# Linear attention into a spectral mixer: the last mode sum and its copies in halves, an eleventh unit for GpSimd, and another order of the last outputs

## The chip, the cores and the metric

One core of a Trainium2 chip. The metric is the device time of one execution in microseconds (us), the median of several runs. The engines are TensorE (PE; PEld is its weight load), VectorE (DVE), ScalarE (ACT), GpSimd (POOL) and SyncE (SP, which only issues DMAs here). Sixteen DMA engines move data between the chip's memory and the SBUF; matmul results arrive in PSUM, which holds eight banks of 2 KB per partition.

## The reference

```python
def _attn_ref(q, k, v, w_phi):            # q, k, v: (8, 8, 576, 64), w_phi: (64, 128)
    def phi(x):
        proj = np.einsum('bhsd,df->bhsf', x, w_phi)
        proj = proj - np.max(np.abs(proj), axis=-1, keepdims=True)
        return np.concatenate([np.exp(proj), np.exp(-proj)], axis=-1)
    q_p, k_p = phi(q), phi(k)
    kv = np.einsum('bhsf,bhsd->bhfd', k_p, v)
    z = np.sum(k_p, axis=2)
    num = np.einsum('bhsf,bhfd->bhsd', q_p, kv)
    den = np.einsum('bhsf,bhf->bhs', q_p, z)[..., None] + 1e-06
    return num / den

def _moe_ref(x, w_r, w_i, w_ch):          # x: (8, 576, 512), w_r, w_i: (64, 512, 512)
    X = np.fft.rfft(x, axis=1)
    Y = np.zeros_like(X)
    Xr, Xi = np.real(X[:, :64]), np.imag(X[:, :64])
    Yr = np.einsum('bmd,mde->bme', Xr, w_r) - np.einsum('bmd,mde->bme', Xi, w_i)
    Yi = np.einsum('bmd,mde->bme', Xr, w_i) + np.einsum('bmd,mde->bme', Xi, w_r)
    Y[:, :64] = Yr + 1j * Yi
    y = np.fft.irfft(Y, n=576, axis=1)
    u = x + y
    return u + np.maximum(u @ w_ch, 0.0)
```

The attention's output, with its heads side by side, is the x of the second function. The weights `w_r` and `w_i` are 134 MB in float32; they are read once.

## The kernel before, in words

The kernel has one program for all engines with an order written out by hand.

**Attention.** 32 steps go over pairs of batches or heads. Each step makes the features of q and k, the sums over k, the quotient, and its part of the forward Fourier transform (`x_mm`). The result x stays in the SBUF as `xs_all`, 40 chunks of 128 rows: chunk `b * 5 + c` is rows of batch b, and the fifth chunk of a batch has only 64 rows.

**Mode sums.** 32 of them (k = 0 to 31): `weights(k)` loads a `wr` and a `wi` tile on the GpSimd queue, three sums ahead; `mode_mm` multiplies them with the transformed x into psY; `mode_sum` adds psY to `Yacc`. The sums 24 to 31 are the last ones of their eight groups of modes; there `mode_sum` writes the total as `yst` (bf16), TensorE transposes it into ptY, and VectorE copies ptY into `sY`. The first 22 sums run inside the attention, the others in a loop of their own behind it.

**By batch.** `by_batch(sY, P)` runs after k = 25, 27, 29 and 31 (P = 0 to 3). For its 16 modes it makes two things for each batch: Z, the spectrum times `w_ch` (`mm_z` into psZ), and Y, the spectrum itself (`mm_r` into psR). PSUM holds the batches j = 0 to 3 (and j + 4 in the second half, h = 1) in four groups of 32 partitions. ScalarE copies Z into `zall` and VectorE copies Y into `yall`, where each batch has its own columns and each P its own 32 rows. For P = 3 the copies of batches 0 and 4 go straight there; the others go through the staging tiles `stz` and `sty` and six DMAs of 64 KB, on SP for j = 1 and on GpSimd's queue for j = 2 and 3.

**Work in between.** In the same loop `pieces` transposes two chunks of x (`flip_x`, T3), multiplies them with `w_ch` (`times_w`, psW in T2) and lets ScalarE put the product into `xw`. `reordered` permutes the rows of a pair of chunks of `xs_all` in place: two matmuls into psX (T0 or T1) and one ScalarE copy (L686, L688). It is called up to twice after k <= 24 and after even k, and stops when the pair has not been through `flip_x` yet.

**Output units.** 20 units, four pairs of chunks and one half unit (the 64-row chunks of two batches) for each of b = 0 to 3, that is for batches b and b + 4. A unit adds the inverse transform of Z to `xw` in psB (`add_xw`, `add_z`), ScalarE takes its ReLU; it adds the inverse transform of Y to x in psA (`add_x`, `spec`), and VectorE adds psA to the ReLU. In a "late" unit, whose pair is listed in `late`, x does not go through TensorE: GpSimd adds the reordered x at the end (L778). psB and psA of even and odd units lie in T2, T3 and T0, T1. The outputs are issued on SP (L856); `lag` says how many units later the issue stands. The groups b = 1 and b = 2 write four chunks with one DMA, b = 0 and b = 3 two.

Four PSUM tags, T0 to T3, of two banks each, hold everything behind the attention. An access waits for the earlier accesses of the same tile that it depends on.

Of the kernel before, what the change touches and what calls it, by code (L numbers as in the profile page):

```python
# [10 lines left out]
F32 = mybir.dt.float32  # L11
F32R = mybir.dt.float32r
BF16 = mybir.dt.bfloat16
I32 = mybir.dt.int32
ACT = mybir.ActivationFunctionType
ALU = mybir.AluOpType
AX = mybir.AxisListType

B_, H_, S_, D_ = 8, 8, 576, 64
NMODES = 64  # L20
DMODEL = 512
# [5 lines left out]
def kernel(  # L27
# [11 lines left out]
    nc = tc.nc  # L39
# [4 lines left out]
    psum = psum_cm.__enter__()  # L44
    pw = ctx.enter_context(tc.tile_pool(name="pw", bufs=3))

    ident_b = const.tile([128, 128], BF16, name="ident_b")
# [8 lines left out]
    Yacc = pers.tile([128, 8, DMODEL], F32, name="Yacc")  # L56
# [333 lines left out]
    def mode_mm(k, tag="yr"):  # L390
        g, gi = groups[k]
        XT = XTs[1 - g if k < 8 else g % 2]
        wt = W.pop(k)
        if gi < 0:
            psY = psum.tile([128, 2, DMODEL], F32, name="psY2", tag="pC", bufs=1)
            for par in range(2):
                for ri in range(2):
                    for j in range(4):
                        for x in range(2):
                            r = slice(64 * x, 64 * x + 64)  # L400
                            m = 16 * (-1 - gi) + 8 * x + 2 * j + par
                            c0 = (16, 0, 48, 32)[2 * ri + par]
                            nc.tensor.matmul(
                                psY[32 * j:32 * j + 32, x, :],
                                lhsT=XT[r, c0:c0 + 32, m],
                                rhs=wt[ri][r, 2 * j + par, :],
                                start=(par == 0 and ri == 0), stop=(par == 1 and ri == 1),
                            )
            return psY
        psY = psum.tile([128, DMODEL], F32, name="psY", tag=tag, bufs=1)  # L410
        for par in range(2):
            for ri in range(2):
                for j in range(4):
                    m = 8 * gi + 2 * j + par
                    c0 = (16, 0, 48, 32)[2 * ri + par]
                    nc.tensor.matmul(  # L416
                        psY[32 * j:32 * j + 32, :],
                        lhsT=XT[:, c0:c0 + 32, m],
                        rhs=wt[ri][:, 2 * j + par, :],
                        start=(par == 0 and ri == 0), stop=(par == 1 and ri == 1),  # L420
                    )
        return psY

    def mode_sum(k, psY, pb=None):
        g, gi = groups[k]
        if gi < 0:
            G = -1 - gi
            if g == 0:
                nc.vector.tensor_copy(Yacc[:, 2 * G:2 * G + 2, :], psY)
            else:  # L430
                nc.vector.tensor_tensor(
                    out=Yacc[:, 2 * G:2 * G + 2, :], in0=psY, in1=Yacc[:, 2 * G:2 * G + 2, :],
                    op=ALU.add)
        elif g < 3:
            nc.vector.tensor_tensor(  # L435
                out=Yacc[:, gi, :], in0=psY, in1=Yacc[:, gi, :], op=ALU.add)
        else:
            yst = pb.tile([128, DMODEL], BF16, name="yst", tag="yst", bufs=2)
            nc.vector.tensor_tensor(out=yst, in0=psY, in1=Yacc[:, gi, :], op=ALU.add)
            return yst  # L440


# [76 lines left out]
    psY = None  # L519
# [3 lines left out]
    with tc.manual_schedule():  # L523
# [25 lines left out]
        for n in range(N + 2):  # L549
# [9 lines left out]
            if psY is not None:  # L559
                mode_sum(k_out, psY)  # L560
                psY = None
# [70 lines left out]

    yall = pb.tile([128, B_, DMODEL], BF16, name="yall", bufs=1)
    zall = pb.tile([128, B_, DMODEL], BF16, name="zall", bufs=1)
    xw = pb.tile([128, B_ * NCH - N_EARLY, DMODEL], BF16, name="xw", bufs=1)


# [2 lines left out]
    copies = []  # L642
# [20 lines left out]
    def pieces(n):  # L663
        for _ in range(n):
# [7 lines left out]
                copies.pop(0)()  # L672


    late = {0: ((1, 0), (1, 2)), 1: ((0, 0), (1, 0), (1, 2)), 2: ((0, 0), (1, 0), (1, 2)),
            3: ((0, 0), (0, 2))}
    reorder = sorted((b + 4 * x) * NCH + c for b in range(4) for x, c in late[b])

    def reordered(tag):
# [10 lines left out]

    def by_batch(sY, P):
        cols = [sY[:, dc].rearrange("p g c -> p (g c)") for dc in range(4)]
        psZ = psum.tile([128, 2, DMODEL], F32, name="psZ", tag="T0")
        psR = psum.tile([128, 2, DMODEL], F32, name="psR", tag="T1")

        def mm_z(h):
            for dc in range(4):
                for j in range(4):
                    nc.tensor.matmul(psZ[32 * j:32 * j + 32, h, :], lhsT=cols[dc][:, j + 4 * h::8],  # L699
                                     rhs=wchb[:, dc, :], start=(dc == 0), stop=(dc == 3))  # L700

        def mm_r(h):
            for dc in range(4):
                for j in range(4):
                    nc.tensor.matmul(
                        psR[32 * j:32 * j + 32, h, dc * 128:(dc + 1) * 128],
                        lhsT=cols[dc][:, j + 4 * h::8], rhs=ident_b, start=True, stop=True)

        rows = slice(32 * P, 32 * P + 32)

        def copy(j):
            r = slice(32 * j, 32 * j + 32)
            nc.scalar.copy(zall[rows, j::4, :], psZ[r])
            nc.vector.tensor_copy(yall[rows, j::4, :], psR[r])  # L714

        if P < 3:
            for f in (mm_z, mm_r):
                for h in range(2):
                    f(h)
            copies.extend([lambda j=j: copy(j) for j in range(4)])  # L720
            return

        stz, sty = [pb.tile([128, 2, DMODEL], BF16, name=nm, bufs=1) for nm in ("stz", "sty")]
        for h in range(2):
            mm_z(h)
            mm_r(h)
            nc.scalar.copy(zall[rows, 4 * h, :], psZ[0:32, h, :])
            nc.vector.tensor_copy(yall[rows, 4 * h, :], psR[0:32, h, :])  # L730
        nc.scalar.copy(stz, psZ)
        nc.vector.tensor_copy(sty, psR)
        for j in range(1, 4):
            for dst, src in ((zall, stz), (yall, sty)):
                (nc.sync if j == 1 else nc.gpsimd).dma_start(
                    dst[rows, j::4, :], src[32 * j:32 * j + 32])

# [43 lines left out]
    with tc.manual_schedule():  # L783
        plan = {22: 3, 23: 3, 24: 2, 25: 2, 26: 2, 27: 1, 28: 2, 29: 1, 30: 1, 31: 0}
        while k_out < 32:
            k = k_out
            gi = groups[k][1]
            while k_in < min(k_out + NW, 32):
                weights(k_in)
                k_in += 1  # L790
            if k == 31:
                add_xw(u0)
            yst = mode_sum(k, mode_mm(k, "T3"), pb)
            k_out += 1
            if yst is not None:
                if ahead:
                    times_w()
                pt = psum.tile([128, 4, 128], BF16, name="ptY", tag="T3" if k < 31 else "T1")
                for dc in range(4):
                    nc.tensor.transpose(pt[:, dc, :], yst[:, dc * 128:(dc + 1) * 128], ident_b)  # L800
                if k == 31:
                    add_x(u0)
                if gi % 2 == 0:
                    sY = pb.tile([128, 4, 2, 128], BF16, name="sY", tag="sY")
                nc.vector.tensor_copy(sY[:, :, gi % 2, :], pt)
                if gi % 2 == 1:
                    by_batch(sY, gi // 2)
            pieces(plan[k])
            if k <= 24 or k % 2 == 0:
                assert not copies  # L810
                for tag in ("T0", "T1"):
                    if reorder:
                        reordered(tag)
            if k == 30:
                times_w()
        assert not todo and not ahead and not reorder and not copies

    units = []
    for b in range(4):
# [4 lines left out]
        for x in range(2):  # L824
            out_v = out[b + 4 * x].rearrange("(p n) e -> p n e", n=9)
            for c in (0, 2):
# [8 lines left out]
        u4 = dict(bc=((b, 4), (b + 4, 4)), o=o4, late=False, half=True, lag=0,  # L835
                  dmas=[(out[b + 4 * x].rearrange("(p n) e -> p n e", n=9)[:, 4, :],
                         o4[64 * x:64 * x + 64]) for x in range(2)])
        units += [u4] + us if b == 3 else us + [u4]
    units[0].update(psA=u0["psA"], psB=u0["psB"])

    with tc.manual_schedule():
        for n, u in enumerate(units):
            u["tags"] = ("T2", "T3") if n % 2 == 0 else ("T0", "T1")
        for n in range(len(units) + 3):
            if n < len(units):
                u = units[n]
                if n:
                    add_xw(u)
                add_z(u)
                if n:  # L850
                    add_x(u)
                spec(u)
            for lag in (3, 1, 0):
                if 0 <= n - lag < len(units) and units[n - lag]["lag"] == lag:
                    for dst, src in units[n - lag]["dmas"]:
                        nc.sync.dma_start(dst, src)  # L856


# [28 lines left out]
```

## Time and profile before

| | |
|---|---|
| median of 3 runs | 457.19 us (456.78, 457.19, 460.01) |
| profiled execution | 456.96 us, its span 455.2 us |
| busy in the span | TensorE 305.3 us (67%), VectorE 295.8 (65%), ScalarE 261.2 (57%), GpSimd 196.9 (43%) |
| moved by DMA | 97.70 MB, mean 215 GB/s as written; memory reads 163.64 MB |
| GpSimd adds L778 | 10 of 2.13 us, 425.4 to 448.8 |
| final adds L774 | 16 of 1.22 us and 4 of 0.68 us, 421.15 to 448.9 |
| last output issue on SP | 451.59 us |

The span runs from the first to the last instruction of the profiled execution; 1.76 us lie around it. A row of a timeline has the start, the time from the first start to the last end, the engine, the line, the operation, the output and inputs, the shapes, the number of instructions, and in brackets the idle time before it with what ended it. A row of the chain has the start, its length and what it was. A row of the stretches has the window, its length, the busy time and number of instructions of each engine, the granted TensorE clock, the mean busy share of the DMA engines (it can read above 1) and the rate.

### The profile page before, as it was taken

What the parts mean: (1) busy time and instruction counts of PE and PEld (TensorE: products, weight loads), DVE (VectorE), ACT (ScalarE), POOL (GpSimd) and SP (SyncE); (2) the same over time, 40 slices, a digit from 0 to 9 for tenths busy, and PEclk for the clock granted to TensorE, in tenths of its full rate; (3) what the DMA queues carried; (4) which work ended last, traced back from release to release, by engine and by line L of the source; (5) the groups of instructions that cost most, each with busy time, mean ns of one, the idle gap of its engine ahead of it and who ended that gap; (6) DMA issues with size and microseconds to landing.
All of it is one profiled execution on the core that took longest, in us unless ns stands there. A gap on an engine that the chain in (4) does not pass through costs nothing.

```text
span 455.2 us, 11075 instructions
## 1 busy us (share of the span) xinstructions
PE 305.3 (67%) x4637; PEld 199.0 (44%) x4637; DVE 295.8 (65%) x417; ACT 261.2 (57%) x528; POOL 196.9 (43%) x250
## 2 busy tenths in 40 slices
PE   3476686745676676657564554776678878867993
PEld 2364565633554554534443332543344445444441
DVE  6588789847988788876657472776422362654873
ACT  4576877833676877865545452766224455554662
POOL 4956576445564356644344341444011311100793
PEclk9998889876779879996678685988899999999998
DMA  6999999999999999999999999999999999990787
GB/s 182 191 229 222 225 216 226 221 206 225 216 225 218 229 219 227 220 221 223 222 208 219 219 218 218 207 208 208 207 207 207 207 207 208 206 187 15 242 325 299
DMA packets 84034, 97.70 MB, mean 215 GB/s; under 512 B 3281, under 2 KB 77265, under 8 KB 83473
## 3 DMA queue, kind: packets, MB, share of 16 engines
q0 software_dynamic: 75728, 76.75, 101.4%
q1 hardware_dynamic: 8096, 20.19, 12.6%
q8 instruction: 36, 0.59, 0.5%
q14 instruction: 14, 0.11, 0.1%
q10 hardware_dynamic: 160, 0.07, 0.1%
HBM read 163.64 MB, written 9.44 MB: 380 GB/s over the span
## 4 chain that ended last, share of the span: by engine, by line
DMA 30%; PE 24%; DVE 24%; ACT 8%; issue 6%; POOL 5%; SPq 1%; DVEq 0%; ACTq 0%; POOLq 0%
DMA wi<-in_moe_w_i_dram 14%; DMA k<-in_k_dram 6%; DVE mkq L233 6%; PE psW L659 6%; DMA wr<-in_moe_w_r_dram 5%; DMA q<-in_q_dram 5%; DVE xs_all L336 3%; DVE nd L322 3%; DVE tB L315 3%; ACT AA L240 2%; PE psY L416 2%; POOL vaug L270 2%; PE psZ L699 2%; DVE yall L714 2%; ACT e L262 2%
## 5 line engine op out<-in xcount | busy, mean ns | idle before, releaser
L270 POOL TENSOR_TENSOR vaug<-vn,ee 128x576 bf16<-128x576 f32 x64 | 72.8, 1156 | 57.2 <-ACT ee L255 45.7
L240 ACT ACTIVATE AA<-psT 128x1024 bf16<-128x1024 f32 x64 | 62.0, 1021 | 42.8 <-PE psT L208 42.3
L162 POOL DMA_DIRECT2D wr<-in_moe_w_r_dram x24 | 21.9, 912 | 114.2 <-PE psY L416 107.9
L262 ACT ACTIVATE e<-mkq 64x4 f32<-64x4 f32 (+1 forms) x128 | 26.3, 206 | 63.1 <-DVE mkq L233 60.8
L244 ACT ACTIVATE AA<-psk 128x1024 bf16<-128x1024 f32 x64 | 61.4, 1009 | 0.0
L416 PE MATMUL psY<-wi,XT 128*32 128x512 bf16 x192 | 24.8, 464 | 25.0 <-DMA wi<-in_moe_w_i_dram 25.0
L416 PEld LDWEIGHTS <-XT 128*32 128x32 bf16 x384 | 17.7, 167 | 51.9 <-issue 43.4
L233 DVE TENSOR_REDUCE mkq<-psk 128x8 f32<-128x1024 f32 x32 | 38.8, 1213 | 1.0 <-PE psk L199 0.9
L233 DVE TENSOR_REDUCE mkq<-psq 128x8 f32<-128x1024 f32 x32 | 38.9, 1217 | 0.5 <-PE psq L199 0.4
L435 DVE TENSOR_TENSOR Yacc<-psY,Yacc 128x512 f32<-128x512 f32 x16 | 11.0, 689 | 42.2 <-PE psY L416 42.2
L661 ACT CAST xw<-psW 128x1024 bf16<-128x1024 f32 x17 | 17.2, 1012 | 36.4 <-PE psW L659 30.5
L286 PE MATMUL kvz<-vaug,AA 64*128 64x65 bf16 x1152 | 29.7, 212 | 11.4 <-POOL vaug L275 10.1
L190 DVE COPY kT<-ptr 128x640 bf16<-128x640 bf16 x32 | 15.7, 492 | 32.4 <-PE ptr L184 32.4
L416 PE MATMUL psY<-wr,XT 128*32 128x512 bf16 x192 | 24.5, 469 | 16.3 <-DMA wr<-in_moe_w_r_dram 7.5
L315 DVE TENSOR_TENSOR tB<-psNB,e 128x650 f32<-128x650 f32 x32 | 26.7, 833 | 11.6 <-PE psNB L305 11.0
L659 PE MATMUL psW<-wchb,sT 128*128 128x512 bf16 x136 | 32.2, 379 | 2.1 <-ACT xw L661 2.1
L286 PEld LDWEIGHTS <-AA 64*128 64x128 bf16 x1152 | 25.6, 108 | 16.2 <-issue 12.4
L305 PEld LDWEIGHTS <-AA 128*128 128x128 bf16 x640 | 28.7, 109 | 8.8 <-issue 8.5
L336 DVE TENSOR_TENSOR xs_all<-nd,rden 128x640 bf16<-128x640 f32 x32 | 29.5, 921 | 1.1
L208 PE MATMUL psT<-qT,w 64*128 64x512 bf16 x64 | 15.4, 471 | 21.0 <-DVE mkq L233 21.0
L322 DVE TENSOR_TENSOR nd<-psNA,tB 128x650 f32<-128x650 f32 x32 | 26.7, 835 | 4.1 <-DVE tB L315 0.5
L184 PE MATMUL ptr<-ident_b,k 128*128 128x128 bf16 x160 | 17.6, 254 | 14.8 <-DVE qT L190 13.0
(135 smaller groups left out, 712.2 us busy)
## 6 DMA issues: line engine op xcount, KB each, us to landing
wr<-in_moe_w_r_dram POOLq DMA_DIRECT2D x24, 1024.0 KB, 23.6
wi<-in_moe_w_i_dram POOLq DMA_DIRECT2D x24, 1024.0 KB, 27.8
wr<-in_moe_w_r_dram POOLq DMA_DIRECT2D x16, 512.0 KB, 16.1
wi<-in_moe_w_i_dram POOLq DMA_DIRECT2D x16, 512.0 KB, 19.4
vn<-in_v_dram SPq DMA_DIRECT2D x24, 288.0 KB, 5.6
out_dram<-of SPq DMA_DIRECT2D x16, 256.0 KB, 2.4
out_dram<-of SPq DMA_DIRECT2D x8, 512.0 KB, 3.7
q<-in_q_dram POOLq DMA_DIRECT2D x12, 288.0 KB, 20.0
```

Of the source, the lines that this page charges most:

```text
L233: nc.vector.tensor_reduce(out=o, in_=i, axis=AX.X, op=ALU.max, apply_absolute_value=True)
L240: nc.scalar.activation(AA[:, 0, ab, 0:1024].rearrange("f (x j p) -> f j x p", j=2, p=64), st["psT"].rearrange("f j (x p) -> f j x p", p=64 ...
L244: nc.scalar.activation(AA[:, 1, ab, 0:1024].rearrange("p (c j f) -> p j c f", c=4, j=2), st["psk"], ACT.Exp, scale=sc)
L262: nc.scalar.activation(e2[64 * jj:64 * jj + 64, hh, 0:NCH - jj], mkq[64 * hh:64 * hh + 64, 1, 5 * jj:5 + 4 * jj], ACT.Exp, scale=2.0)
L270: nc.gpsimd.tensor_tensor(out=vaug[:, ab, :, 0:64], in0=st["v"], in1=ee[:, ab, :].unsqueeze(2).to_broadcast([128, 9, D_]), op=ALU.mult,)
L286: nc.tensor.matmul(kvz[:, hh, ab * 65:(ab + 1) * 65], lhsT=AA[r, 1, ab, 128 * j:128 * j + 128], rhs=vaug[r, ab, j, :], start=(j == 0), sto ...
L305: nc.tensor.matmul(p[:, hh, 65 * c:65 * c + 65], lhsT=AA[:, 0, ab, x:x + 128], rhs=kvzF[:, hh, ab * 65:(ab + 1) * 65], start=True, stop=True,)
L315: nc.vector.tensor_tensor(out=tB, in0=st["psNB"], in1=e2.unsqueeze(3).to_broadcast([128, 2, NCH, 65]), op=ALU.mult,)
L322: nc.vector.tensor_tensor(out=nd, in0=st["psNA"], in1=st["tB"], op=ALU.add)
L336: nc.vector.tensor_tensor(out=xo, in0=nd[:, :, :, 0:64], in1=rden.to_broadcast([128, 2, NCH, 64]), op=ALU.mult,)
L416: nc.tensor.matmul(psY[32 * j:32 * j + 32, :], lhsT=XT[:, c0:c0 + 32, m], rhs=wt[ri][:, 2 * j + par, :], start=(par == 0 and ri == 0), sto ...
L659: nc.tensor.matmul(ps[:, x, :], lhsT=sT[:, x, dc, :], rhs=wchb[:, dc, :], start=(dc == 0), stop=(dc == 3))
```

## The change

- `mode_mm` runs over `ri` (wr or wi) in its outer loop and over the parity of the mode in its inner one.
- At k = 31 `mode_sum` adds in two halves of 256 columns into two tiles; the transposes go into two PSUM tiles (T0 and T1) and each is copied on its own.
- `yall` and `zall` become two halves of one tile `zy`. `by_batch` no longer has psZ and psR: there is one tile for each half h of the batches, with Z in its first bank and Y in its second. For P < 3 ScalarE copies Z and Y of the first half, VectorE those of the second. For P = 3 the order of the matmuls stays; the staging tile of the first half is copied by ScalarE as soon as that half is there, that of the second by VectorE, and each DMA moves Z and Y of one batch.
- `late[0]` gains (0, 2): an eleventh late unit, and an eleventh pair to reorder.
- The half unit of b = 3 is the last unit instead of the first of its group.
- From the last unit's step on, the second output of a unit is issued on ScalarE's queue.

```diff
-        for par in range(2):
-            for ri in range(2):
+        for ri in range(2):
+            for par in range(2):
                 for j in range(4):
...
-            yst = pb.tile([128, DMODEL], BF16, name="yst", tag="yst", bufs=2)
-            nc.vector.tensor_tensor(out=yst, in0=psY, in1=Yacc[:, gi, :], op=ALU.add)
+            cuts = [0, DMODEL] if k < 31 else [0, DMODEL // 2, DMODEL]
+            yst = []
+            for a, b in zip(cuts, cuts[1:]):
+                t = pb.tile([128, b - a], BF16, name="yst", tag="yst" if k < 31 else f"yst{a}",
+                            bufs=2 if k < 31 else 1)
+                nc.vector.tensor_tensor(out=t, in0=psY[:, a:b], in1=Yacc[:, gi, a:b], op=ALU.add)
+                yst += [t[:, x:x + 128] for x in range(0, b - a, 128)]
...
-    late = {0: ((1, 0), (1, 2)), 1: ((0, 0), (1, 0), (1, 2)), 2: ((0, 0), (1, 0), (1, 2)),
-            3: ((0, 0), (0, 2))}
+    late = {0: ((0, 2), (1, 0), (1, 2)), 1: ((0, 0), (1, 0), (1, 2)),
+            2: ((0, 0), (1, 0), (1, 2)), 3: ((0, 0), (0, 2))}
...
-        psZ = psum.tile([128, 2, DMODEL], F32, name="psZ", tag="T0")
-        psR = psum.tile([128, 2, DMODEL], F32, name="psR", tag="T1")
+        ps = [psum.tile([128, 2, DMODEL], F32, name="psZY", tag=f"T{h}") for h in range(2)]
...
-        def copy(j):
-            r = slice(32 * j, 32 * j + 32)
-            nc.scalar.copy(zall[rows, j::4, :], psZ[r])
-            nc.vector.tensor_copy(yall[rows, j::4, :], psR[r])
+        def copy(j, h, eng):
+            eng(zy[rows, :, j + 4 * h, :], ps[h][32 * j:32 * j + 32])
 
         if P < 3:
-            for f in (mm_z, mm_r):
-                for h in range(2):
-                    f(h)
-            copies.extend([lambda j=j: copy(j) for j in range(4)])
+            for h in range(2):
+                mm_z(h)
+                mm_r(h)
+            copies.extend([lambda j=j: (copy(j, 0, nc.scalar.copy),
+                                        copy(j, 1, nc.vector.tensor_copy)) for j in range(4)])
             return
-        stz, sty = [pb.tile([128, 2, DMODEL], BF16, name=nm, bufs=1) for nm in ("stz", "sty")]
         for h in range(2):
             mm_z(h)
             mm_r(h)
-            nc.scalar.copy(zall[rows, 4 * h, :], psZ[0:32, h, :])
-            nc.vector.tensor_copy(yall[rows, 4 * h, :], psR[0:32, h, :])
-        nc.scalar.copy(stz, psZ)
-        nc.vector.tensor_copy(sty, psR)
-        for j in range(1, 4):
-            for dst, src in ((zall, stz), (yall, sty)):
+            nc.scalar.copy(zall[rows, 4 * h, :], ps[h][0:32, 0, :])
+            nc.vector.tensor_copy(yall[rows, 4 * h, :], ps[h][0:32, 1, :])
+            st = pb.tile([128, 2, DMODEL], BF16, name=f"st{h}", bufs=1)
+            (nc.vector.tensor_copy if h else nc.scalar.copy)(st, ps[h])
+            for j in range(1, 4):
                 (nc.sync if j == 1 else nc.gpsimd).dma_start(
-                    dst[rows, j::4, :], src[32 * j:32 * j + 32])
+                    zy[rows, :, j + 4 * h, :], st[32 * j:32 * j + 32])
...
-                pt = psum.tile([128, 4, 128], BF16, name="ptY", tag="T3" if k < 31 else "T1")
-                for dc in range(4):
-                    nc.tensor.transpose(pt[:, dc, :], yst[:, dc * 128:(dc + 1) * 128], ident_b)
+                if gi % 2 == 0:
+                    sY = pb.tile([128, 4, 2, 128], BF16, name="sY", tag="sY")
+                for a, b, tag in ((0, 4, "T3"),) if k < 31 else ((0, 2, "T0"), (2, 4, "T1")):
+                    pt = psum.tile([128, b - a, 128], BF16, name="ptY", tag=tag)
+                    for dc in range(a, b):
+                        nc.tensor.transpose(pt[:, dc - a, :], yst[dc], ident_b)
+                    nc.vector.tensor_copy(sY[:, a:b, gi % 2, :], pt)
                 if k == 31:
                     add_x(u0)
...
-        units += [u4] + us if b == 3 else us + [u4]
+        units += us + [u4]
...
-                    for dst, src in units[n - lag]["dmas"]:
-                        nc.sync.dma_start(dst, src)
+                    for x, (dst, src) in enumerate(units[n - lag]["dmas"]):
+                        (nc.scalar if x and n >= len(units) - 1 else nc.sync).dma_start(dst, src)
```

More of the change, by code (lines that the diff above doesn't have):

```diff
@@ L630 @@
     psum = ctx.enter_context(tc.tile_pool(name="psumT", bufs=1, space=bass.MemoryType.PSUM))
-    yall = pb.tile([128, B_, DMODEL], BF16, name="yall", bufs=1)
-    zall = pb.tile([128, B_, DMODEL], BF16, name="zall", bufs=1)
+    zy = pb.tile([128, 2, B_, DMODEL], BF16, name="zy", bufs=1)
+    zall, yall = zy[:, 0], zy[:, 1]
     xw = pb.tile([128, B_ * NCH - N_EARLY, DMODEL], BF16, name="xw", bufs=1)
@@ L698, in mm_z @@
                 for j in range(4):
-                    nc.tensor.matmul(psZ[32 * j:32 * j + 32, h, :], lhsT=cols[dc][:, j + 4 * h::8],
+                    nc.tensor.matmul(ps[h][32 * j:32 * j + 32, 0, :], lhsT=cols[dc][:, j + 4 * h::8],
                                      rhs=wchb[:, dc, :], start=(dc == 0), stop=(dc == 3))
@@ L705, in mm_r @@
                     nc.tensor.matmul(
-                        psR[32 * j:32 * j + 32, h, dc * 128:(dc + 1) * 128],
+                        ps[h][32 * j:32 * j + 32, 1, dc * 128:(dc + 1) * 128],
                         lhsT=cols[dc][:, j + 4 * h::8], rhs=ident_b, start=True, stop=True)
         rows = slice(32 * P, 32 * P + 32)
-        def copy(j):
-            r = slice(32 * j, 32 * j + 32)
-            nc.scalar.copy(zall[rows, j::4, :], psZ[r])
-            nc.vector.tensor_copy(yall[rows, j::4, :], psR[r])
+        def copy(j, h, eng):
+            eng(zy[rows, :, j + 4 * h, :], ps[h][32 * j:32 * j + 32])
         if P < 3:
-            for f in (mm_z, mm_r):
-                for h in range(2):
-                    f(h)
-            copies.extend([lambda j=j: copy(j) for j in range(4)])
+            for h in range(2):
[3 more added lines that the diff above has]
+                                        copy(j, 1, nc.vector.tensor_copy)) for j in range(4)])
             return
-        stz, sty = [pb.tile([128, 2, DMODEL], BF16, name=nm, bufs=1) for nm in ("stz", "sty")]
         for h in range(2):
@@ L797 @@
                     times_w()
-                pt = psum.tile([128, 4, 128], BF16, name="ptY", tag="T3" if k < 31 else "T1")
-                for dc in range(4):
-                    nc.tensor.transpose(pt[:, dc, :], yst[:, dc * 128:(dc + 1) * 128], ident_b)
+                if gi % 2 == 0:
[5 more added lines that the diff above has]
+                    nc.vector.tensor_copy(sY[:, a:b, gi % 2, :], pt)
                 if k == 31:
                     add_x(u0)
-                if gi % 2 == 0:
-                    sY = pb.tile([128, 4, 2, 128], BF16, name="sY", tag="sY")
-                nc.vector.tensor_copy(sY[:, :, gi % 2, :], pt)
                 if gi % 2 == 1:
```

## The prediction

> Unit numbers below follow the last loop of the changed program: u0 to u4 for batches 0 and 4, u5 to u9, u10 to u14, u15 to u19; the fifth of each group is the 64-row unit, which the kernel before runs first in the last group.
>
> **What bounds the kernel now.** I read the stretches first, then the chain that ended last, then the timeline of each engine from 395 us on, then the output tiles.
>
> ```profile
> core 0: us, PE busy (x) PEld busy (x) DVE busy (x) ACT busy (x) POOL busy (x), PEclk, DMA share, GB/s
> 395.00:405.00 10.00, 8.68 (x124) 5.36 (x123) 4.28 (x6) 5.36 (x6) 0.00 (x0) 1.00 1.24 208
> ...
> 412.00:420.00 8.00, 6.11 (x92) 3.63 (x92) 2.95 (x5) 2.25 (x4) 0.00 (x0) 1.00 0.02 4
> ...
> 430.00:440.00 10.00, 9.82 (x53) 4.13 (x53) 7.94 (x8) 7.27 (x8) 8.67 (x5) 1.00 0.83 320
> ```
>
> Up to 405 the DMA engines are full (share 1.24) with weights. From 412 to 420 they are idle: nothing is loaded any more and nothing is ready to be written. From 420 the output units run and TensorE is busy 98%. Every edit that can matter lies behind 340 us.
>
> ```profile
> 349.50 1.89 PE psW L659 x8
> 351.39 0.43 PE psX L686 x2
> 351.82 1.05 PE psY L416 x15
> ...
> 411.27 1.02 ACT xw L661
> 412.30 0.04 issue
> 412.34 0.59 PE psB L751 x2
> 412.93 1.08 PE psY L416 x14
> 414.01 0.02 issue
> 414.03 0.70 DVE yst L439
> ```
>
> The chain shows that from 343 us to the last mode sum TensorE, VectorE and ScalarE hand work to each other and no link is a DMA. The last `wi` load is issued at 388.70 and takes 24.3 us, so it lands at about 413.0: compute and load arrive together, and the load is at most 0.15 us from being the bound.
>
> ```profile
> 417.46 1.09 PE L699 MATMUL psZ<-wchb,sY 128*32 128x512 bf16 x16 [0.43 <-ACT zall L729]
> ...
> 419.18 1.01 ACT L731 CAST stz<-psZ 128x1024 bf16<-128x1024 f32 x1
> 419.53 1.23 DVE L732 CAST sty<-psR 128x1024 bf16<-128x1024 f32 x1
> 420.09 1.03 ACT L760 ACTIVATE of<-psB 128x1024 f32<-128x1024 f32 x1
> ```
>
> In the last `by_batch` the second half of Z waits for a copy of the first half, 0.43 us, though the two halves are different banks of psZ. Both staging copies stand ahead of the first ReLU (420.09) and the first final add (421.15).
>
> ```profile
> L774 DVE TENSOR_TENSOR of<-psA,of x16: 1224/1224/1225, 421.2 to 447.6; 128x1024 f32<-128x1024 f32 x16
> L778 POOL TENSOR_TENSOR of<-of,xs_all x10: 2122/2128/2141, 425.4 to 446.7; 128x1024 f32<-128x1024 f32 x10
> ```
>
> ```profile
> 447.00:448.00 1.00, 0.40 (x2) 0.00 (x0) 0.55 (x2) 0.60 (x1) 1.00 (x1) 1.00 0.34 131
> 448.00:449.00 1.00, 0.00 (x0) 0.00 (x0) 0.86 (x1) 0.00 (x0) 0.84 (x1) 1.00 0.70 283
> 449.00:450.00 1.00, 0.00 (x0) 0.00 (x0) 0.00 (x0) 0.00 (x0) 0.00 (x0) 1.00 1.01 402
> ```
>
> GpSimd's ten adds fill 21 of the last 27 us. All computing is over at 448.9, yet the span ends at 455.2: from 448.3 to 453.5 the DMA engines write about 2.1 MB at 400 GB/s with share 1.0, after a hole of about 1 us at 447.4, in which the in-order SP queue waited for VectorE (issue at 447.21, first bytes 1.1 us later).
>
> **The change, part by part.**
>
> *One more reordered pair.* (0,2) joins `late`, so `reordered` runs eleven times. Counting its slots (two at k = 22, 23, 24, 26, 28, 30, held back by `todo`), the new pair fills the slot left free at k = 23, just ahead of the 351.39 row. It costs two L686 matmuls, 0.43 us on the chain, and an L688 copy of 1.01 us on ScalarE, which is idle 1.38 us before its next xw copy; bounds 0 and 1.01, I take 0.43. No later link waits for weights, so all of it reaches the last sum: +0.43.
>
> *Mode sums, `wr` first.* At the last sum `wi` is there at 413.0 and the sum would now start at 413.29: nothing to gain. Earlier sums lie under the full DMA. Bounds -0.2 to 0.2, taken 0.
>
> *Last sum in halves.* From 512 columns (0.69) and 1024 columns (1.22) an add of 256 is about 0.43 us; from copies of 0.42 and 0.69 a ptY copy of 256 is 0.29; two transposes, from 0.40 for four and 0.61 for eight, 0.29. Two adds end 0.87 us after psY, at 414.90 in old times; the first copy ends at 415.20, the second at 415.55. TensorE has the two L766 matmuls until 415.5, then `mm_z` may start on the first two column groups, against 415.69: -0.19 (bounds -0.08, if it waits for both copies, and -0.25).
>
> *psZ and psR by halves.* The second `mm_z` writes its own tile, so its 0.43 us wait goes. From the rows, `mm_z` and `mm_r` of a half take 1.32 us from start to start: the second half begins at 416.82 instead of 417.46 and ends at 418.15 instead of 418.79.
>
> *Copies.* ScalarE: zall 0.57 from 416.86, first staging tile 1.01, second zall 0.57, so its first ReLU starts at 419.0 instead of 420.09. VectorE: yall 0.68 from 416.86, yall 0.68 from 418.17, second staging tile 1.23 to 420.10, first final add at 420.12 instead of 421.15: -1.03. This needs ScalarE and VectorE to read different banks of one tile at the same time. No row shows two engines doing so; the price if they may not is the first rival. Six 64 KB DMAs stay six, land in 2.1 to 2.3 us and are first read at unit 5, over 3 us later. On SP the outputs of unit 0, and on GpSimd the first add, stand behind the issues that wait for the second staging tile; both come later anyway.
>
> *The eleventh late unit.* Unit 1 loses two matmuls (0.43 us of TensorE) and gives GpSimd 2.13 us. Walking u0 to u4 with four PSUM buffers, u5 starts on TensorE at 424.5 in old times, against 425.92: -1.42, with the 0.43 from k = 23 -1.0. GpSimd gets u1 at 423.0, where it idled to 425.40 before, is then nearly never idle, and ends u13 at 442.6 instead of 443.58: -1.0. Units u5 to u14 have the same work and keep that distance.
>
> *Half unit last, two queues.* The half unit (eight matmuls, a 0.60 ReLU, a 0.68 add, two 128 KB writes) moves behind four units and behind ten issues on SP. VectorE's last add ends at about 447.1 instead of 448.9. The last five units' outputs are now 2.36 MB, behind the 1.05 MB of u13 that SP issues at 442.7. First bytes at 443.8; 3.15 MB at 0.40 MB/us are 7.9 us, and 0.26 MB in 2 KB rows 0.9 us (stretches with such rows show 273 to 313 GB/s): 452.6, against 453.5 now, the hole of 1 us being filled but 0.26 MB added. SP's pitch is 0.626 us for each 256 KB issue and the transfer takes 0.65, so a second issuing queue hardly helps. Behind the last byte lie 1.7 us, as before.
>
> The Trainium skill, "DMA: Bandwidth & Descriptors", section "Issuing engines are not separate DMA queues", says the same of the last edit: issues from another engine end on the same 16 DMA engines and save only sequencer time. The trace agrees, with share 1.01 at 402 GB/s in 449 to 450 us; by the rule the two-queue edit alone is worth 0.
>
> **Sum.** +0.43 - 0.19 - 0.45 (wait) - 0.39 (copies: the rest of 1.03) - 0.40 (unit 1) = -1.0 at u13; the burst behind it gives +0.1: span 454.3 against 455.2. The profiled execution took 456.96 (1.76 around the span), 0.23 below the median of 457.19. So **456.1**, with 455 to 457 as its own range.
>
> **Rivals.**
>
> *Readers of one tile take turns (slower).* The row at 417.46 shows that the program already orders accesses to different banks of one tile. If it does so for two readers, the chain is zall 416.86 to 417.43 on ScalarE, yall to 418.14, staging tile to 419.18, zall to 419.77, yall to 420.48, staging tile on VectorE to 421.72. The first add starts at 421.73, 0.58 later than now, u5 about 0.14, and with k = 23 0.6 later; u13 ends on GpSimd at 444.2. Burst: 444.3 + 1.1 + 8.8 + 1.7 = 455.9, +0.7: 457.7. It decides as soon as either engine waits for the other's read. For it: that row. Against it: the row is a write behind a read, not two reads. The Trainium skill, "PSUM — Partial Sum Buffer", section "PSUM bank collisions raise a hardware error", has it that only accesses to the same bank and quadrant collide, reads included, and that different banks run clean; by that rule the turns are not needed, but no run here shows what the program orders.
>
> *The burst is not held by the transfer.* Slices of 430 GB/s occur at 440 to 442. If the rows of the last units go faster, or the second queue keeps more in flight, issues end it: u13 at 442.7, then ten slots of which SP has eight more; the last SP issue is at 449.1, lands 2.4 later, plus 1.25: 452.75, -2.45, so 454.5. Against it: share 1.0 throughout the last burst.
>
> *The halves give nothing back before unit 5.* If the ScalarE copy of the new pair sits on the chain (1.01 instead of 0.43) and `mm_z` waits for both copies, 0.7 is lost: 456.8.
>
> **Chances.** Forecast 0.42, turns 0.33, free burst 0.12, nothing given back 0.08; 0.05 for a larger stall. The range 454.3 to 458.8 takes in the free burst and the turns with 1 us for the spread of runs (456.78 to 460.01). One per cent, about what a measurement of this kernel can tell, is 4.6 us: none of the cases reaches it, which leaves 0.03 for faster, 0.06 for slower (the stall), 0.91 between.
>
> **What would show it.** After: the second `mm_z` without idle time; psY of the last sum at 413.3; ScalarE's and VectorE's reads of the first half side by side (turns: end to end), and the first final add 2.0 us after the end of the second half (turns: 3.6); eleven L778 adds with GpSimd idle under 1 us from the first on; two 128 KB writes last; DMA share 1.0 without a hole from 444 on and a last byte near 452.6. A first ReLU later than 420.5 would make the forecast wrong, so would a hole in the last burst, or a mode sum that waits for weights.

## The result, and the profile after

| | before | after |
|---|---|---|
| median of 6 runs each, on one chip | 457.32 us (456.78 to 460.01) | 462.83 us (461.17 to 464.47) |
| profiled execution | 456.96 us, span 455.2 | 461.29 us, span 459.5 |
| first add of the last mode sum (`yst<-psY,Yacc`) | 414.03 | 413.95 |
| from there to the span's end | 41.17 us | 45.55 us |

The change makes the kernel slower: ratio 1.0097, 95% interval 1.0070 to 1.0124. The forecast was 456.1 us (454.3 to 458.8); the measured time lies above that range, at the edge of the 1% by which the chances were told apart.

The third and fourth rows show where the time went. The last mode sum starts 0.08 us earlier than before, and behind it the changed kernel takes 4.38 us longer. (The sum came no later only because this execution reached psY of k = 22 1.31 us earlier, at 330.20 against 331.51; how early that is differs from execution to execution.) In the 45 us behind the sum the DMAs that write the output tell the story. The first fence is the timeline of SP after the change (two windows of it), the second that of ScalarE's own issues, the third the list of SP's waits (engine and line, what it waited for: us in total, times, longest).

```profile
443.82 0.48 SPq L861 DMA_DIRECT2D out_dram<-of  x1
...
450.36 1.89 SPq L861 DMA_DIRECT2D out_dram<-of  x3
```

```profile
448.00 0.53 ACTq L861 DMA_DIRECT2D out_dram<-of  x1
448.57 0.61 ACTq L861 DMA_DIRECT2D out_dram<-Yacc  x1
```

```profile
SPq L861 <- DMA out_dram<-of: 6.0, 1, 6.0
```

SP issues the first 512 KB output of u13 at 443.82, almost where it was issued before (443.71), and then stands for 6.0 us. Before the change all ten of the last outputs went out from there in 8.47 us, with one long wait, 2.2 us for VectorE:

```profile
443.71 8.47 SPq L856 DMA_DIRECT2D out_dram<-of  x10
```

What SP waits for after the change is no engine but another output DMA. Behind the waiting output eight more stand in SP's order, and the very last unit was finished by 448.57, when ScalarE issued its second write. In the stretches with the SP filter (window, length, granted clock, DMA share, GB/s) the DMA engines run dry meanwhile and then catch up at the rate known from before. (The granted clock falls to 0.50 only after TensorE's last matmul.)

```profile
446.00:447.00 1.00, 1.00 0.07 25
447.00:448.00 1.00, 1.00 0.00 0
448.00:449.00 1.00, 1.00 0.00 0
454.00:455.00 1.00, 0.50 1.00 397
```

The timing gives the cause away. ScalarE's first output issue stands at 448.00: it is the second 256 KB of u16, which GpSimd's last add ends at 447.97. It takes 2.3 us to land, that is until 450.3, and at 450.36 SP goes on. The semaphores that the trace records with each issue say why an SP issue should wait for a DMA that ScalarE issues. (A semaphore is a counter by which a DMA reports its end.) The DMAs of SP and of ScalarE use one set of eight semaphores, 100 to 107, handed out in turn, and an issue waits until the earlier DMA on its semaphore has landed. With all outputs on SP that earlier DMA is an SP issue eight places before, landed long ago. ScalarE's two issues carry 103 and 105. These are places among the outputs of u8, which carry 102 and 104 and which SP issues at 436.84 and 437.37, far ahead of when ScalarE's run. So the second output of u13 has to wait for the first ScalarE output, on 103, which landed at 450.34. The second output of u17 has to wait for the other one, on 105; that had landed at 450.97, before SP came to it at 451.52, so it costs nothing more here.

The staging part did not go as forecast either. These are the rows of the last `by_batch` from TensorE, VectorE and ScalarE, after the change:

```profile
413.21 0.70 PE L416 MATMUL psY<-wi,XT 128*32 128x512 bf16 x8 [0.43 <-DMA wi<-in_moe_w_i_dram]
415.42 1.10 PE L705 MATMUL psZY<-wchb,sY 128*32 128x512 bf16 x16
...
416.57 1.04 PE L705 MATMUL psZY<-wchb,sY 128*32 128x512 bf16 x16
```

```profile
413.95 0.76 DVE L444 TENSOR_TENSOR yst<-psY,Yacc 128x256 bf16<-128x256 f32 x2 [4.11 <-PE psY L416]
...
417.40 0.68 DVE L734 CAST zy<-psZY 32x512 bf16<-32x512 f32 x1 [2.02 <-ACT zy L733]
419.76 0.68 DVE L734 CAST zy<-psZY 32x512 bf16<-32x512 f32 x1 [1.67 <-ACT zy L733]
420.46 1.23 DVE L736 CAST st<-psZY 128x1024 bf16<-128x1024 f32 x1
421.60 2.35 DVE L777 TENSOR_TENSOR of<-psA,of 128x1024 f32<-128x1024 f32 x2
```

```profile
416.80 0.57 ACT L733 CAST zy<-psZY 32x512 bf16<-32x512 f32 x1 [5.28 <-PE psZY L711]
418.12 1.01 ACT L736 CAST st<-psZY 128x1024 bf16<-128x1024 f32 x1 [0.75 <-DVE zy L734]
419.16 0.57 ACT L733 CAST zy<-psZY 32x512 bf16<-32x512 f32 x1
```

The second `mm_z` has no wait left. But the copies run end to end: VectorE's copy of Y starts when ScalarE's copy of Z ends (417.40), ScalarE's staging copy when that one ends (418.12), and so on. The brackets name the other engine's read of the same PSUM tile, though Z and Y lie in different banks of it. These are waits of the program: the trace records with VectorE's copy at 417.40 a wait for ScalarE's semaphore, and with ScalarE's at 418.12 one for VectorE's. That both engines now write into one SBUF tile, `zy`, is not the reason. ScalarE's staging copy does not write `zy` and waits all the same, and an earlier `by_batch`, where each engine reads a PSUM tile of its own, has both writing into `zy` at once, from 407.39 to 408.10 (a row of ScalarE and one of VectorE):

```profile
406.08 2.02 ACT L718 CAST zy<-psZY 32x1024 bf16<-32x1024 f32 x2
407.39 2.46 DVE L718 CAST zy<-psZY 32x1024 bf16<-32x1024 f32 x2
```

The first final add starts 7.65 us after the last sum's first add, against 7.12 before, where its row was

```profile
421.15 2.44 DVE L774 TENSOR_TENSOR of<-psA,of 128x1024 f32<-128x1024 f32 x2 [0.39 <-ACT of L760]
```

### The profile page after: what moved, and what is told of

Read it like the earlier page. It is cut to its first block, busy times and chain, and to the rows that moved or that the text cites. A ratio compares the mean times of both kernels' runs of the same rounds, so it can differ in the third digit from the quotient of the medians.

```text
span 459.5 us, 11056 instructions
## 1 busy us (share of the span) xinstructions
PE 303.0 (66%) x4619; PEld 199.8 (43%) x4637; DVE 296.6 (65%) x419; ACT 261.9 (57%) x529; POOL 199.7 (43%) x251
## 4 chain that ended last, share of the span: by engine, by line
DMA 40%; issue 18%; DVE 16%; PE 10%; POOL 8%; ACT 4%; SPq 1%; DVEq 0%; POOLq 0%; ACTq 0%
DMA wi<-in_moe_w_i_dram 29%; DMA k<-in_k_dram 6%; DVE mkq L233 5%; DMA q<-in_q_dram 4%; DVE xs_all L336 2%; DVE nd L322 2%; DVE tB L315 2%; POOL vaug L270 2%; ACT AA L240 1%; ACT of L763 1%; POOL wi L162 1%; PE ptr L184 1%; PE psB L754 1%; POOL wr L162 1%; PE psNB L305 1%
## 5 line engine op out<-in xcount | busy, mean ns | idle before, releaser
L416 PE MATMUL psY<-wi,XT 128*32 128x512 bf16 x192 | 18.3, 441 | 27.3 <-DMA wi<-in_moe_w_i_dram 27.3
L305 PEld LDWEIGHTS <-AA 128*128 128x128 bf16 x640 | 29.7, 111 | 7.0 <-issue 6.5
L162 POOL DMA_DIRECT2D wi<-in_moe_w_i_dram x24 | 21.1, 880 | 23.7 <-PE psY L416 20.8
L416 PE MATMUL psY<-wr,XT 128*32 128x512 bf16 x192 | 17.5, 435 | 16.5 <-DMA wr<-in_moe_w_r_dram 7.8
```

The costliest lines, as they stand in the source:

```text
L162: nc.gpsimd.dma_start(t, w[8 * gi:8 * gi + 8, g * 128:(g + 1) * 128, :].rearrange("m p e -> p m e"))
L305: nc.tensor.matmul(p[:, hh, 65 * c:65 * c + 65], lhsT=AA[:, 0, ab, x:x + 128], rhs=kvzF[:, hh, ab * 65:(ab + 1) * 65], start=True, stop=True,)
L416: nc.tensor.matmul(psY[32 * j:32 * j + 32, :], lhsT=XT[:, c0:c0 + 32, m], rhs=wt[ri][:, 2 * j + par, :], start=(par == 0 and ri == 0), sto ...
```

## The experiments

The start of the last sum varies between executions (its first add stands at 413.95 to 419.06; in gpsimd_queue's, the latest, the granted clock was 0.50 from 330 to 340 us). Behind it TensorE's granted clock is 1.0 up to its last matmul. So besides the ratio of times each kernel is compared by the **stretch** from that first add to the span's end. A stretch is read from one profiled execution, with spans given to 0.1 us, and what the change does ahead of the last sum is not in it. A ratio is to the kernel before on the same chip.

| kernel | ratio (95% interval) | stretch, us |
|---|---|---|
| before | 1 | 41.17 |
| after | 1.0097 (1.0070 to 1.0124) | 45.55 |
| all_sp | 1.0002 (0.9978 to 1.0027) | 41.51 |
| before_two_queues | 1.0099 (1.0069 to 1.0129) | 46.25 |
| gpsimd_queue | 1.0018 (0.9996 to 1.0040) | 41.94 |
| act_last_only | 1.0085 (1.0059 to 1.0110) | 44.67 |
| no_turns_sp | 0.9965 (0.9944 to 0.9987) | 40.26 |
| no_turns_ten_sp | 0.9992 (0.9961 to 1.0022) | 40.49 |
| no_turns_half_first | 0.9982 (0.9958 to 1.0005) | 40.13 |
| no_turns_split | 0.9971 (0.9944 to 0.9999) | 39.71 |
| split_half_first | 0.9964 (0.9939 to 0.9989) | 39.84 |
| split_half_first_late | 0.9943 (0.9919 to 0.9967) | 39.41 |

### Is it the second queue?

**all_sp**: the changed kernel with every output on SP.

```diff
-                        (nc.scalar if x and n >= len(units) - 1 else nc.sync).dma_start(dst, src)
+                        nc.sync.dma_start(dst, src)
```

> The changed kernel with every output issued on SP again, nothing else undone. In the changed kernel's trace SP stands still for 6.0 us between the first and the second output of unit 13 and goes on when an output that ScalarE issued has landed. Theory A (a completion semaphore shared by the two issuing queues makes SP wait for ScalarE's output): the 6 us go, SP issues back to back from 443.8, the last output starts near 451.7, span near 455.4, time about 457.2, that is within 1 us of the kernel before. Theory B (the burst is late for another reason: unit 13's GpSimd add, the order of the last units, slow transfers): the hole stays and the time is 460 or more.

The stretch falls from 45.55 to 41.51 and the time is that of the kernel before. Two outputs put back on SP are worth 4.04 us. From 440 us on no output issue of SP waits for a DMA, and its outputs follow each other:

```profile
443.86 7.29 SPq L861 DMA_DIRECT2D out_dram<-of  x10
451.24 1.18 SPq L861 DMA_DIRECT2D out_dram<-Yacc  x2
```

**before_two_queues**: the kernel before with that one edit alone.

```diff
-                    for dst, src in units[n - lag]["dmas"]:
-                        nc.sync.dma_start(dst, src)
+                    for x, (dst, src) in enumerate(units[n - lag]["dmas"]):
+                        (nc.scalar if x and n >= len(units) - 1 else nc.sync).dma_start(dst, src)
```

> The kernel before with only the two-queue edit: from the last unit's step on the second output of a unit is issued on ScalarE's queue. Theory A: three outputs go to ScalarE and the semaphores they take are those that SP's outputs of units 13 and the half unit need, so SP stands still from about 441 to 450; the last SP issue is near 455, time 460 to 461.5, 3 to 4.5 us slower than before. Theory B (two queues are harmless): within 0.5 us of the kernel before, or up to 0.5 us faster.

The edit alone costs as much as the whole change: 1.0099, some 4.5 us, and 5.08 us in the stretch, where 3 to 4.5 were expected. There the order of units is that of before, so three outputs go to ScalarE (at 450.50 to 453.75), and SP waits for output DMAs three times:

```profile
SPq L856 <- DMA out_dram<-of: 8.9, 3, 6.8
```

**gpsimd_queue**: the changed kernel with GpSimd in ScalarE's place. In the trace GpSimd's DMAs have semaphores of their own, 110 to 117, so this keeps a second issuing queue and takes away the sharing.

```diff
-                        (nc.scalar if x and n >= len(units) - 1 else nc.sync).dma_start(dst, src)
+                        (nc.gpsimd if x and n >= len(units) - 1 else nc.sync).dma_start(dst, src)
```

> The changed kernel with the second output of the last issues on GpSimd's queue instead of ScalarE's. Theory A: GpSimd's DMAs use completion semaphores of their own, so SP does not wait: span near 455 to 455.5, time 456.5 to 457.3, about as with one queue, because the transfers of the last burst fill the DMA engines. Theory B (a second queue as such delays the burst): the hole of several us stays and the time is 460 or more.

1.0018, stretch 41.94, and SP does not wait for an output DMA from the last units at all. It is a little slower than all_sp (0.43 us in one execution each). So not the second queue itself costs 4 us, but the waits that ScalarE's share of SP's semaphores brings.

**act_last_only**: only the last 128 KB of all goes to ScalarE.

```diff
-                        (nc.scalar if x and n >= len(units) - 1 else nc.sync).dma_start(dst, src)
+                        (nc.scalar if x and n >= len(units) - 1 and lag == 0 else nc.sync).dma_start(dst, src)
```

> The changed kernel with a single output, the second 128 KB of the last half unit, on ScalarE's queue; all others on SP. Theory A (shared completion semaphores, handed out in an order in which ScalarE's issue stands early): one write is enough. SP stands still again, now ahead of the second output of unit 17, from about 446.7 until ScalarE's write, issued near 448.5, has landed near 450.8; the span comes to about 458.5 to 459.5, the time to 460 to 461.5, nearly the whole loss. Rival (ScalarE's two writes take the DMA engines or the issue slots from SP): 128 KB cost 0.3 us at most, time as with SP alone.

One small write is enough: 1.0085, 3.16 us more than all_sp in the stretch. The wait moved as the semaphores say it must: it is now for the one remaining ScalarE DMA, issued at 449.38 and on the same semaphore, 104, as the output that waits. SP goes on 2.3 us later.

```profile
447.10 0.47 SPq L861 DMA_DIRECT2D out_dram<-of  x1
...
451.70 0.47 SPq L861 DMA_DIRECT2D out_dram<-of  x1
```

```profile
SPq L861 <- DMA out_dram<-Yacc: 4.1, 1, 4.1
```

### Do two readers of one tile take turns?

**no_turns_sp**: all_sp, with one engine for all reads of a half: ScalarE copies Z and Y of the first half with one instruction, VectorE those of the second.

```diff
-            nc.scalar.copy(zall[rows, 4 * h, :], ps[h][0:32, 0, :])
-            nc.vector.tensor_copy(yall[rows, 4 * h, :], ps[h][0:32, 1, :])
+            (nc.vector.tensor_copy if h else nc.scalar.copy)(zy[rows, :, 4 * h, :], ps[h][0:32])
```

> The changed kernel with every output on SP, and in the last by_batch one engine alone reads each half: ScalarE copies Z and Y of batch 0 together and then the staging tile of the first half, VectorE the same for the second half. If the turns of the two engines at one tile cost what I worked out (0.6 us at the first final add, and more where ScalarE waits), the first final add comes about 1 us earlier than in the changed kernel, near 420.6, unit 5 about 1 us earlier, and the time is 0.7 to 1.5 us below the same kernel with turns. If the turns are hidden by something else, the two are equal within 0.3 us.

VectorE now waits only for TensorE:

```profile
418.91 1.22 DVE L733 CAST zy<-psZY 32x1024 bf16<-32x1024 f32 x1 [2.54 <-PE psZY L711]
420.14 1.23 DVE L735 CAST st<-psZY 128x1024 bf16<-128x1024 f32 x1
421.28 2.35 DVE L776 TENSOR_TENSOR of<-psA,of 128x1024 f32<-128x1024 f32 x2
```

With the last sum's first add at 414.94 there, the first final add comes 6.34 us behind it (7.65 after the change, 7.12 before). The stretch falls by 1.25 us (41.51 to 40.26), within the 0.7 to 1.5 that were expected; the intervals of the two ratios just overlap. One instruction in place of two also saves each engine 0.14 us of copying, so a small part of the 1.25 need not be the turns. Without them and without the second queue the change is faster than before: 0.9965.

### What are the other parts worth?

**no_turns_ten_sp**: no_turns_sp without the eleventh late unit.

```diff
-    late = {0: ((0, 2), (1, 0), (1, 2)),
+    late = {0: ((1, 0), (1, 2)),
```

> The version with all outputs on SP and one reading engine for each half, but with ten late units: (0, 2) goes back to TensorE and is not reordered. If the eleventh late unit saves TensorE's two matmuls on the path, unit 5 and the end come 0.3 to 0.5 us later here, counted from the last mode sum. If GpSimd is the bound with eleven adds, unit 13 is out earlier here and the end is equal or up to 0.5 us earlier.

The first issue of u13 stands 28.98 us behind the first add instead of 28.56, and 0.23 us of that is left in the stretch. That agrees with the forecast of -0.40 at u13; the ratios (0.9992 and 0.9965) point the same way but their intervals overlap.

**no_turns_half_first**: no_turns_sp with the half unit of the last group first, as in the kernel before.

```diff
-        units += us + [u4]
+        units += [u4] + us if b == 3 else us + [u4]
```

> The version with all outputs on SP and one reading engine for each half, but with the half unit of the last group first again. My sum gave the new order nothing but the fill of a hole of 1 us against 0.26 MB more in the last burst, so the end should lie within 0.4 us of the version with the half unit last. If the order is worth something, the end is 0.5 to 1.5 us later here.

40.13 against 40.26: moving the half unit is worth nothing that can be told. A measured ratio of 0.9982, whose interval holds both 0.9965 and 1, adds no more.

### A better version

What is left at the end is a burst that waits for its first data. In no_turns_sp the DMA engines are not full just before it; these are stretches with the POOL filter (window, length, GpSimd's busy time and instructions, granted clock, DMA share, GB/s):

```profile
443.00:444.00 1.00, 1.00 (x2) 1.00 0.64 189
444.00:445.00 1.00, 1.00 (x1) 1.00 0.45 188
445.00:446.00 1.00, 1.00 (x2) 1.00 1.06 442
```

Group b = 2 writes two units' chunks with one DMA, so bytes that are ready wait for the second unit. **no_turns_split** lets it write each unit on its own, as b = 0 and b = 3 do.

```diff
-        whole = b in (1, 2)
+        whole = b == 1
```

> The version with all outputs on SP and one reading engine for each half, and the third group's outputs written as two chunks for each unit instead of four for two units, so that unit 12's half need not wait for unit 13's GpSimd add. The trace of that version shows the DMA engines half idle from 443 to 445 (share 0.64 and 0.45) in front of the last burst. If the burst behind unit 13 sets the end, 0.5 MB leave 2.1 us earlier, the hole is filled and the end comes 0.5 to 1.0 us earlier. If the issue pitch of SP sets the end, two more issues cost up to 1.2 us.

The stretch falls by 0.55 us, to 39.71; the ratio (0.9971) is that of no_turns_sp within the intervals. Two more kernels build on it: **split_half_first** has the half unit first again, **split_half_first_late** also moves a late place of the group b = 2 from its last unit, (1, 2), to (0, 2), so that the last output of that group no longer waits for GpSimd:

```diff
-            2: ((0, 0), (1, 0), (1, 2)), 3: ((0, 0), (0, 2))}
+            2: ((0, 0), (0, 2), (1, 0)), 3: ((0, 0), (0, 2))}
```

> All outputs on SP, one reading engine for each half, the third group's outputs by unit, and the half unit of the last group first again. Alone, the split made the stretch from the last mode sum's first add to the end 0.55 us shorter and the half unit first 0.13 us. If both act on the same last burst by taking bytes out of it, they add up: about 39.6 us for that stretch, against 41.2 in the kernel before, and a time 0.3 to 0.5% below it. If the hole in front of the burst was the only thing to win, the half unit's order is worth nothing more: 39.7 to 39.9 us.

> The same, and in the third group (0, 2) is a late unit instead of (1, 2), so that its last unit does not go through GpSimd. If the burst is held up by unit 13's GpSimd add, which ends 3 us after VectorE's, its 0.5 MB leave about 3 us earlier and the end comes another 0.5 to 1 us earlier, 38.7 to 39.2 us for the stretch. If the burst is bound by the bytes that are left when VectorE ends, it stays at 39.6.

The half unit first did not add to the split: 39.84 in place of an expected 39.6, so 0.13 us slower than the split alone, where the same move had been 0.13 us faster above; neither is told from nothing. With the late units of b = 2 earlier, GpSimd has 1.36 us to spare before its last two adds, against 1.08 in split_half_first:

```profile
444.96 4.22 POOL L780 TENSOR_TENSOR of<-of,xs_all 128x1024 f32<-128x1024 f32 x2 [1.36 <-DVE of L776]
```

The stretch is 39.41. That lies between the two expected values, 38.7 to 39.2 and 39.6, so what holds up the burst is not settled by it.

The ratio, 0.9943 (0.9919 to 0.9967), is the best of all kernels here: 455.87 us against 458.27 for the kernel before on the same chip, and 1.76 us less in the stretch. Its interval overlaps those of the three versions it is built from.

## Why the prediction was wrong, by its own steps

- **The step that failed is "half unit last, two queues"**, in the sentence that a second issuing queue hardly helps, and in the 0 that was put in the sum for it. The step asked what the second queue could gain (0.626 us of issue against 0.65 of transfer) and bounded the edit from that side only. It did not ask what SP's later issues would then wait for. Measured: +4.04 us in the changed kernel, +5.08 alone. The Trainium skill, "DMA: Bandwidth & Descriptors", section "Issuing engines are not separate DMA queues", was cited for the 0. The row that the prediction set beside it has one queue only; gpsimd_queue has outputs of two queues under way from 455 to 456 us and agrees (share 1.03, 389 GB/s). But the rule is about what can be gained, and these runs show a loss beside it. The prediction named "a hole in the last burst" as what would make it wrong; the hole is 446 to 449 us. The 0.05 kept for a larger stall was all the weight the true outcome had.
- **The copies, forecast -1.03 for the first final add: wrong, and the first rival was right.** The add came 0.53 us later (7.65 against 7.12), where the rival had 0.58. u5's final add came 0.29 later (14.31 us behind the first add, against 14.02), where the rival had about 0.14. Of the rival's price for the end, +0.7, 0.43 is the reordered pair, which lies ahead of the stretch; the 0.27 that are left stand against +0.34 in all_sp. Without the turns the forecast's direction is right and the gain about three quarters of it: the first final add comes 0.78 earlier, not 1.03, and u5's 1.02, where 1.42 had been worked out for its start.
- **One more reordered pair, +0.43: right, though the changed kernel's own profile hides it.** From psY of k = 22 to that of k = 24 the chain takes 20.66 us after and 20.24 before, +0.42; with ten late units (no_turns_ten_sp) it is 20.24 again. Three executions with eleven late units have the full clock and no wait for weights from k = 22 on (act_last_only, no_turns_half_first, no_turns_split). In them the last psY comes 81.73 to 81.76 us behind that of k = 22, against 81.35 before, so the cost does reach the last sum. In the changed kernel's execution "no later link waits for weights" did not hold: TensorE had the `wr` half done and waited 0.43 us for the last `wi` (the bracket at 413.21), the load that the prediction had seen 0.15 us from being the bound. The other eleven profiles show no wait there.
- **Last sum in halves, -0.19**: 413.95 to 415.42 is 1.47 us, against 1.66 before. Right. **The wait of `mm_z`**: gone; the halves start 1.15 us apart, where 1.32 had been worked out and 1.77 was measured before. Right.
- **The eleventh late unit, -0.40 at u13**: 0.42 in the pair no_turns_ten_sp and no_turns_sp. Right, though only 0.23 of it reached the end.
- **The burst**: from u13's first issue to the span's end 11.49 us before and 11.64 in all_sp; the forecast of +0.1 stands, once nothing holds SP back.

The whole sum, -1.0 us, counts +0.43 ahead of the last sum, so behind it the forecast is -1.43 at u13 and, with the burst, -1.33 at the end. In no_turns_sp, without the failed step and without the turns, u13's first issue comes 1.12 us earlier and the end 0.91. The direction is right and the size about two thirds; that 0.91 is close to 1.0 is chance. The sum also ends a little low by its own terms: 454.3 + 1.76 + 0.23 is 456.3, not 456.1. The changed kernel's stretch is that of no_turns_sp with the two measured differences added back: 40.26 + 1.25 + 4.04 = 45.55.

What stays open: whether the chip itself would let two engines read two banks of one tile at once. The program orders these reads, and a kernel without that order was not run. The rule cited for the rival, the Trainium skill's "PSUM — Partial Sum Buffer", section "PSUM bank collisions raise a hardware error", which lets different banks run side by side, is so neither borne out nor refuted here. Nor was a kernel run with ScalarE's DMAs on semaphores apart from SP's; GpSimd's queue stands in for it. The last 0.1 to 0.4 us between the best versions, one profiled execution each, are not told apart.

## What to carry to other kernels

A DMA moved to another queue must be priced by what later issues of the old queue will wait for: look in the trace of the moved version for an issuing engine that waits for a DMA, and see whether that DMA was issued elsewhere. In an order written by hand, a late issue on a second queue can hold up a whole queue of finished work. When two engines copy out of one PSUM tile, count their reads end to end unless a trace shows them side by side, and give each engine a tile of its own where the halves arrive one after the other.

## What the runs showed of the hardware and the program that was not expected

- One 128 KB write issued from ScalarE's queue in place of SP's cost 3.16 us at the end of the kernel, since an SP issue waited 4.1 us for it; two such issues, 256 and 128 KB, cost 4.04 us, with one wait of 6.0. SP's and ScalarE's issues shared semaphores 100 to 107. The same outputs on GpSimd's queue brought no such wait.
- Reads of two banks of one PSUM tile by ScalarE and VectorE were ordered end to end in the built program, though both only read: the arrangement without them is 1.25 us shorter in this stretch. Two engines that wrote into one SBUF tile were not ordered so (406.08 to 409.85).
- The last weight load and TensorE's chain arrive so close together that either can set the last sum: TensorE waited 0.43 us for `wi` in the changed kernel's execution, and no such wait is shown in the other eleven.
